# Computing K and Q of a half together in two PSUM banks, with the stationary tokens loaded once per column tile

## The chip, the cores and the metric

The kernel runs on one core of a Trainium2 chip. The metric is device time in microseconds (us), and a comparison uses fast runs only. (A run is called slow when it is over 1.5% above the fastest of the same kernel.) The record names three chips for the experiments and does not name that of the first pair. The same kernel differed between these three chips by up to 1.5% (means of the kernel before: 1052.4, 1063.3 and 1068.6 us), so every experiment is compared with runs of the kernel before that were made in the same rounds on the same chip. In the profiles PE is TensorE (matmuls), PEld its weight loads, DVE is VectorE, ACT ScalarE and POOL GpSimd; PSUM (`ps` in the traces) is the memory that the kernel's matmuls write to.

## The reference, cut to what matters

```python
# part A: recurrent attention over 64 segments, 32 heads of 128, model width 512
for s in range(64):
    h = concat([mem, x[32*s : 32*s+32]])            # 8 memory rows + 32 rows of x
    q, k, v = h @ Wq, h @ Wk, h @ Wv                # each 512 -> 32 x 128
    p = softmax(mask(q @ k.T * scale))
    o = (p @ v) @ Wo                                # 4096 -> 512
    mem = o[:8]                                     # the next segment needs these
    outs.append(o[8:])
# part B: independent local attention with a memory branch (num / den);
# out = g * A + (1 - g) * B
```

Segment s+1 needs the memory rows of segment s. The kernel therefore has one long serial loop, and it fills the gaps of part A with pieces of part B.

## The kernel before: the parts that matter

The kernel records operations per engine. Each one waits, before its first instruction, for what it reads, and for the last readers of what it overwrites. It allocates PSUM as eight banks of 512 columns (lines 247 to 250), which are tracked as resources.

```python
class Banks:
    def take(self, long=False):            # first fit in a list, oldest returned first (cut)
        ...
    def give(self, *bks):                  # back in the list when the *reading* op is recorded
        for b in bks: self.free.append(b)

# Prog._mk_deps, for a written resource:
#     deps += [r.w] and all of r.readers   (a bank: whoever last copied it out)
```

`give` is called when the program is recorded, not when the reader has run. A bank in the list can therefore still be waiting for its reader on the chip, and the op that takes it inherits that wait.

```python
A_ORDER = """
    Q1 K0 Q0 K1 V0 TK0 TQ0 S0 bP bP TQ1 TK1 bS V1 M0 S1 N0 Fc M1 PV0 E0a N1 E0b Fc PV1 E1b E1a
    W0 W1 WT bS bT Ff Ff Ff bS bP bS""".split()

def proj(bk, lhs, w_sb, b, split, reads, name):      # one pass: 16 matmuls of 512 columns
    def f(pe):
        for c in range(C):                           # 4 chunks of the width 512
            for j in range(4):                       # 4 column tiles of 32
                w = w_sb[:, c, 2048 * b:2048 * (b + 1)]
                ins = pe.matmul(pb[bk][SEG*j:SEG*(j+1), :], lhs(c), cols(w, j) if split else ...,
                                start=(c == 0), stop=(c == C - 1))
    P.op("pe", f, reads=reads, writes=[rbank[bk]], name=name)

def nat_pass(m, b, eng):                             # units K0 K1 Q0 Q1 V0 V1
    bk = B.take()
    proj(bk, lhs, w_sb, b, m != "V", ...)
    evac(eng, nat[:, b, :], pb[bk], [bk], ...)       # copy to SBUF on ACT or DVE
    B.give(bk)
```

Unit `bT` at the end of a segment runs `BAttn.chain`: matmuls of the memory branch (`bN`) into a bank `nb`, then a run of DVE operations that ends with the product `amem` read from `nb`, or, at the end of each job, a transpose copied to `oTs`.

```python
def chain(self, job, G, ob):
    nb = v.BK.take()
    P.op("pe", fn, ..., writes=[v.rbank[nb]], name="bN" + nm)
    # DVE: reciprocal, gate, adot (reads ob); then + 1e-6, reciprocal, gate ...
    P.op("dve", ... ad, T1 * rd ...); v.BK.give(ob)
    P.op("dve", ... am, T2 * rm ...)                 # "amem": the last reader of nb
    v.BK.give(nb)
```

The softmax here doesn't subtract the row's maximum and nothing guards it: scores larger than these inputs give would overflow.

## Time and profile before

The time before is 1060.99 us (median of 3 runs, 1060.31 to 1063.03). What matters, and where it is read:

| reading | value | view |
|---|---|---|
| TensorE (PE) busy | 923 of 1060 us | page, part 1 |
| one K or Q pass to the next | 0.86 us | PE timeline |
| PE gaps at one place modulo 256 instructions | 84 us in 75 gaps | worked out from the trace |
| half-rate TensorE clock | 82 us | clock records of the trace |

The page of the kernel before: the span, the engines' busy times, the granted TensorE clock in 40 slices, and the instruction queue (packets, MB, share).

```profile
span 1059.6 us, 65320 instructions
PE 923.4 (87%) x30149; PEld 565.4 (53%) x30149; DVE 558.8 (53%) x1198; ACT 586.0 (55%) x1211; POOL 229.2 (22%) x603
PEclk9998999999999989999899999999899999989999
q8 instruction: 236, 3.87, 1.5%
```

PE is the busy engine, and in all 64 segments of the trace its projections stand in the order of `A_ORDER` (Q K Q K V V). Every matmul has a weight load of its own: 30,149 of each.

Its timeline at the start of segment 23 (start, length, engine, line, operation, tiles, count):

```profile
432.77 0.39 PE L706 MATMUL ps<-QTj,KTj 32*128 32x256 bf16 x4
433.09 1.05 PE L862 MATMUL ps<-Wq_sb,hT 128*32 128x512 bf16 x16
433.97 1.04 PE L862 MATMUL ps<-Wk_sb,hT 128*32 128x512 bf16 x16
434.83 1.04 PE L862 MATMUL ps<-Wq_sb,hT 128*32 128x512 bf16 x16
435.69 1.04 PE L862 MATMUL ps<-Wk_sb,hT 128*32 128x512 bf16 x16
```

Read the starts, not the lengths: the ends of matmuls are modelled in this profile, and a pass of "1.05 us" is followed by the next after 0.86. A pass is four rounds of 512 columns in four column tiles at once, so a round takes 216 ns, although each pass also carries 16 weight loads. On PEld the loads of a round start one round ahead of their matmuls, while the round before runs: those of the fourth pass start at 435.48, its matmuls at 435.69.

DVE over the same microseconds:

```profile
432.52 0.31 DVE L868 STREAM_TRANSPOSE hT<-aW_sb 128x128 bf16<-128x128 bf16 x1 [2.54 <-ACT aW_sb L319]
432.76 0.22 DVE L786 RECIPROCAL rden<-ps 128x16 f32<-128x16 f32 x1
...
434.56 0.42 DVE L802 TENSOR_TENSOR amem<-ps,rden 128x256 f32<-128x256 f32 x1
434.91 0.68 DVE L321 CAST QN_sb<-ps 128x512 bf16<-128x512 f32 x1
```

The memory branch's chain is still running on DVE when the projections start. Its last reading of a PSUM bank, `amem`, ends at 434.98, which is 1.9 us after the first projection began. Nothing waits for it, because the pass that takes that bank is the fourth, 2.6 us in.

The second loss of the kernel, in PE's list of waits (engine, line, what it waited for: total us, times, longest) and in its timeline:

```profile
PE ps L899 <- issue: 65.1, 56, 2.3
```

```profile
414.40 1.85 PE L899 MATMUL ps<-Wo_sb,OT_sb 128*32 128x128 bf16 x109
417.93 0.46 PE L899 MATMUL ps<-Wo_sb,OT_sb 128*32 128x128 bf16 x19 [1.68 <-issue]
```

PE stops for 1.68 us in the middle of a run of matmuls that wait for nothing that the profile shows. I numbered all PE instructions of the trace, 60,503 with its semaphore instructions: such gaps fall at one place modulo 256 (positions 193 to 198), 84 us in all. The queue that the page calls `instruction` moved 236 packets of 16 KB, one for each 256 of these instructions, and no two of them overlap in time. So I read the gaps as instruction fetch, and call them fetch stalls. After the 58 stalls of over 0.6 us, the next packet starts 1.1 us after PE has resumed and takes 1.1 us, and PE resumes 1.4 us after a packet has landed (medians). Whether a stall follows went with how fast a block of 256 ran: all 43 blocks that ran in under 2.5 us were followed by one (3.5 us with it, in the mean), 27 of the 60 between 2.5 and 3.4 us, and none of the 103 over 3.6 us.

### The profile page before, as it was taken

To read this page: it belongs to the slowest core of one execution; us is meant where nothing else is said; L and a number is where in the kernel's file an instruction comes from. 1 tells how busy PE (TensorE), PEld (TensorE's weight loads), DVE (VectorE), ACT (ScalarE), POOL (GpSimd) and SP (SyncE) were. 2 spreads that over 40 slices of the span, in tenths; PEclk is the share of its full clock that TensorE was granted. 3 is DMA by queue.
4 is the path that set the end of the run, shared out by engine and by line. 5 is a ranking of instruction groups with operands and counts; after the bars stand their busy time and mean duration, and the time that the engine had idled before them with its cause. 6 is when DMAs were issued, how large, how long until landed. Compare 5 with 4: busy or idle time off the path is not lost.

```text
span 1059.6 us, 65320 instructions
## 1 busy us (share of the span) xinstructions
PE 923.4 (87%) x30149; PEld 565.4 (53%) x30149; DVE 558.8 (53%) x1198; ACT 586.0 (55%) x1211; POOL 229.2 (22%) x603
## 2 busy tenths in 40 slices
PE   7967999898988989889898999899898889988886
PEld 4434555555555545555555565555555555555544
DVE  4655555453554636465465646565464546446433
ACT  4442666565665655656565656665565666544444
POOL 6100222221222122222221222222222212211010
PEclk9998999999999989999899999999899999989999
DMA  8897000000101110000001101000111001000110
GB/s 287 265 323 256 12 13 16 17 17 12 25 14 41 38 34 20 24 15 20 20 20 44 39 22 34 14 25 15 24 40 35 22 19 39 10 14 4 40 33 9
DMA packets 65929, 52.23 MB, mean 49 GB/s; under 512 B 34288, under 2 KB 64120, under 8 KB 64120
## 3 DMA queue, kind: packets, MB, share of 16 engines
q1 hardware_dynamic: 65656, 48.06, 15.5%
q8 instruction: 236, 3.87, 1.5%
q14 instruction: 37, 0.30, 0.1%
HBM read 33.47 MB, written 14.57 MB: 45 GB/s over the span
## 4 chain that ended last, share of the span: by engine, by line
PE 72%; issue 9%; ACT 8%; DVE 6%; DMA 3%; SPq 1%; ACTq 0%; POOL 0%; DVEq 0%
PE ps L862 33%; PE ps L899 17%; PE ps L706 5%; ACT PT L714 4%; PE ps L753 4%; PE ps L582 2%; DVE LN_sb L321 2%; PE ps L1061 2%; PE ps L557 2%; ACT R_sb L1043 2%; PE ps L949 2%; ACT R_sb L1040 2%; DVE Pn_sb L1047 2%; DMA scr_pQd<-stgp 1%; DMA Wo_sb<-in_A_Wo_dram 1%
## 5 line engine op out<-in xcount | busy, mean ns | idle before, releaser
L899 PE MATMUL ps<-Wo_sb,OT_sb 128*32 128x128 bf16 x8192 | 151.8, 229 | 52.5 <-issue 51.3
L714 ACT ACTIVATE PT<-ps 128x1024 bf16<-128x1024 f32 x160 | 160.5, 1023 | 26.2 <-PE ps L706 21.9
L899 PEld LDWEIGHTS ps<-Wo_sb,OT_sb 128*32 128x32 bf16 x8192 | 127.4, 101 | 67.1 <-issue 59.2
L722 POOL TENSOR_SCALAR_AFFINE_SELECT PT<-PT 128x256 bf16<-128x256 bf16 (+1 forms) x224 | 98.8, 441 | 277.0 <-ACT PT L714 269.1
L862 PE MATMUL ps<-Wq_sb,hT 128*32 128x512 bf16 x2048 | 143.9, 396 | 2.8 <-DVE hT L868 1.9
L862 PE MATMUL ps<-Wk_sb,hT 128*32 128x512 bf16 x2048 | 139.0, 387 | 0.0
L319 ACT ACTIVATE KN_sb<-ps 128x512 bf16<-128x512 f32 x128 | 76.4, 597 | 108.6 <-PE ps L862 105.8
L868 DVE STREAM_TRANSPOSE hT<-aW_sb 128x128 bf16<-128x128 bf16 x64 | 19.9, 312 | 219.9 <-ACT aW_sb L319 219.9
L862 PE MATMUL ps<-Wv_sb,hT 128*32 128x512 bf16 x2048 | 134.9, 381 | 0.8 <-ACT V_sb L319 0.8
L319 ACT ACTIVATE OT_sb<-ps 128x320 bf16<-128x320 f32 x256 | 96.9, 430 | 55.4 <-PE ps L1070 54.4
L868 DVE STREAM_TRANSPOSE KT_sb<-KN_sb 128x512 bf16<-128x512 bf16 x128 | 88.4, 690 | 48.9 <-ACT KN_sb L319 48.6
L319 ACT ACTIVATE aW_sb<-ps 128x128 bf16<-128x128 f32 x64 | 17.8, 278 | 149.3 <-PE ps L899 146.1
L868 DVE STREAM_TRANSPOSE QT_sb<-QN_sb 128x512 bf16<-128x512 bf16 x128 | 83.5, 690 | 11.7 <-ACT QN_sb L319 10.6
L1129 POOL COPY OTL<-OT_sb 128x256 bf16<-128x256 bf16 x64 | 25.5, 398 | 295.5 <-ACT OT_sb L319 295.5
L862 PEld LDWEIGHTS ps<-Wk_sb,hT 128*32 128x32 bf16 x2048 | 57.3, 99 | 59.1 <-issue 5.7
L862 PEld LDWEIGHTS ps<-Wq_sb,hT 128*32 128x32 bf16 x2048 | 51.9, 99 | 63.3 <-issue 16.6
L321 DVE CAST V_sb<-ps 128x512 bf16<-128x512 f32 x64 | 44.3, 692 | 74.9 <-PE ps L862 74.9
L862 PEld LDWEIGHTS ps<-Wv_sb,hT 128*32 128x32 bf16 x2048 | 50.4, 96 | 54.4 <-ACT P_sb L1019 9.8
L321 DVE CAST QN_sb<-ps 128x512 bf16<-128x512 f32 x64 | 44.0, 687 | 41.4 <-PE ps L862 41.3
L706 PE MATMUL ps<-QTj,KTj 32*128 32x384 bf16 (+3 forms) x512 | 64.2, 309 | 0.0
L1040 ACT ACTIVATE R_sb<-ps 128x160 f32<-128x160 f32 x128 | 38.9, 304 | 36.6 <-PE ps L1036 36.3
L1047 DVE TENSOR_TENSOR Pn_sb<-P_sb,R_sb 128x160 bf16<-128x160 bf16 x128 | 42.6, 333 | 30.9 <-ACT R_sb L1043 21.9
(117 smaller groups left out, 1424.1 us busy)
## 6 DMA issues: line engine op xcount, KB each, us to landing
Wk_sb<-in_A_Wk_dram SPq DMA_DIRECT2D x4, 1024.0 KB, 7.0
Wq_sb<-in_A_Wq_dram SPq DMA_DIRECT2D x4, 1024.0 KB, 8.6
Wv_sb<-in_A_Wv_dram SPq DMA_DIRECT2D x4, 1024.0 KB, 8.4
Wo_sb<-in_A_Wo_dram SPq DMA_DIRECT2D x4, 1024.0 KB, 10.0
scr_vd<-V SPq DMA_DIRECT2D x16, 136.0 KB, 5.3
Vj<-scr_vd SPq DMA_DIRECT2D x32, 68.0 KB, 2.4
Wo_sb<-in_A_x_dram SPq DMA_DIRECT2D x4, 512.0 KB, 7.4
scr_kTd<-stgk SPq DMA_DIRECT2D x16, 128.0 KB, 6.5
```

The lines of the kernel that those rows point to most:

```text
L319: P.op("act", lambda a: a.activation(dst, src, ACT.Copy), reads=[v.rbank[k] for k in bks], writes=dres, name=name)
L321: P.op("dve", lambda d: d.tensor_copy(dst, src), reads=[v.rbank[k] for k in bks], writes=dres, name=name)
L706: ins = pe.matmul(v.pb[bks[x]][:, o:o + w], KT[e][r, 128 * kc:128 * (kc + 1)], QT[r, q0:q0 + w], start=True, stop=True, tile_position=(r.s ...
L714: P.op("act", lambda a: a.activation(pt[:, :, :], v.ps[:, bks[0]:bks[1] + 1, :], ACT.Exp, scale=v.SCALE_B), reads=[v.rbank[b] for b in bks ...
L722: P.op("gp", lambda g, mv=mv: g.affine_select(mv, mv, [[0, mv.shape[1]], [1, 128]], ALU.is_ge, 0.0, base=0, channel_multiplier=-1), reads= ...
L753: ins = pe.matmul(v.pb[ob][:, o:o + 17], pt[:, x, col:col + 128], V[:, kc, 17 * h:17 * (h + 1)], start=first, stop=True, skip_group_check= ...
L862: ins = pe.matmul(pb[bk][SEG * j:SEG * (j + 1), :], lhs(c), cols(w, j) if split else w[:, 512 * j:512 * (j + 1)], start=(c == 0), stop=(c ...
L868: P.op("dve", lambda d: d.transpose(dst, src), reads=reads, writes=writes, name=name)
L899: ins = pe.matmul(pb[bk][SEG * j:SEG * (j + 1), 0:128], lhs(h), cols(Wo_sb[:, h, :], j), start=(h == 0), stop=(h == H - 1))
L1040: P.op("act", lambda a: a.activation(R_sb[:, b, :], pb[bk][:, 224:384], ACT.Ln), reads=[rbank[bk]], writes=[Rs("R%d" % b)], name="ln%d_%d" ...
L1047: P.op("dve", lambda d: d.tensor_tensor(wide(Pn_sb, b)[:, :, 0:L], wide(P_sb, b)[:, :, 0:L], R_sb[:, b, :].rearrange("p (i q) -> p i q", q ...
L1129: P.op("gp", lambda gq: gq.tensor_copy(OTL[par][:, :, 8 * r:8 * r + 8], OT_sb[:, :, SEG:L]), reads=[Rs("OT%d_%d" % (c, hf)) for c in range ...
```

## The change

Its intent: K and Q of one half multiply the same stationary tokens. If both are computed together in two banks, each column tile loads its tokens once and two matmuls use them. That removes 32 of the 64 K/Q weight loads of a segment. The core of the diff:

```diff
+def matmul_again(nc, pe, first, out, rhs, start, stop):
+    m = first.ins
+    return pe.add_instruction(mybir.InstMatmult(
+        ..., ldweights=False, ..., ins=[pe.lower_ap(rhs), m.ins[1]], outs=[pe.lower_ap(out)], ...))
 A_ORDER = """
-    Q1 K0 Q0 K1 V0 TK0 TQ0 S0 bP bP ...
+    P0 P1 V0 TK0 TQ0 S0 bP bP ...
-A_ENG = dict(K0="act", K1="act", Q0="act", Q1="dve", ...
+A_ENG = dict(K0="act", K1="act", Q0="dve", Q1="act", ...
+    def proj_two(bks, lhs, w_two, b, reads, name):
+        def f(pe):
+            for c in range(C):
+                ...
+                first = [pe.matmul(pb[bks[0]][rows[j], :], lhs(c), w[0][j], ...) for j in range(4)]
+                for j in range(4):
+                    ins = matmul_again(v.nc, pe, first[j], pb[bks[1]][rows[j], :], w[1][j], ...)
+        P.op("pe", f, reads=reads, writes=[rbank[k] for k in bks], name=name)
+        def two_pass(b):
+            bks = [B.take(), B.take()]
+            proj_two(bks, lhs, (Wk_sb, Wq_sb), b, ...)
+            for m, nat, bk in (("K", KN_sb, bks[0]), ("Q", QN_sb, bks[1])):
+                evac(ENG["%s%d" % (m, b)], nat[:, b, :], pb[bk], [bk], ...)
+            B.give(*bks)
```

Note `writes=[rbank[k] for k in bks]`: the pair is one operation, and it waits for both banks before its first matmul.

More of the change, by code (lines that the diff above doesn't have):

```diff
@@ L225, in build @@
     v = NS()
+    v.nc = nc
     _, S, DM = A_x.shape
@@ L365 @@
     pass
+def matmul_again(nc, pe, first, out, rhs, start, stop):
+    m = first.ins
+    return pe.add_instruction(mybir.InstMatmult(
+        start_tensor_calc=start, stop_tensor_calc=stop, tile_size=m.tile_size, tile_position=m.tile_position, ldweights=False,
+        name=nc.get_next_instruction_name(), engine=m.engine, debug=m.debug, ins=[pe.lower_ap(rhs), m.ins[1]], outs=[pe.lower_ap(out)],
+        bass_skip_group_check=True))
 def plan_const(v):
@@ L823 @@
 A_ORDER = """
-    Q1 K0 Q0 K1 V0 TK0 TQ0 S0 bP bP TQ1 TK1 bS V1 M0 S1 N0 Fc M1 PV0 E0a N1 E0b Fc PV1 E1b E1a W0 W1 WT bS bT Ff Ff Ff
+    P0 P1 V0 TK0 TQ0 S0 bP bP TQ1 TK1 bS V1 M0 S1 N0 Fc M1 PV0 E0a N1 E0b Fc PV1 E1b E1a W0 W1 WT bS bT Ff Ff Ff
     bS bP bS""".split()
-A_ENG = dict(K0="act", K1="act", Q0="act", Q1="dve", V0="act", V1="dve", KL0="dve", KL1="dve", QL0="dve", QL1="dve", VL0="dve",
+A_ENG = dict(K0="act", K1="act", Q0="dve", Q1="act", V0="act", V1="dve", KL0="dve", KL1="dve", QL0="dve", QL1="dve", VL0="dve",
              VL1="dve", OL="act", W="act", E0a="act", E0b="act", E1a="act", E1b="act", last=0)
@@ L865, in proj @@
         P.op("pe", f, reads=reads, writes=[rbank[bk]], name=name)
+    def proj_two(bks, lhs, w_two, b, reads, name):
+        def f(pe):
+            ins = None
+            for c in range(C):
+                w = [[cols(w_sb[:, c, 2048 * b:2048 * (b + 1)], j) for j in range(4)] for w_sb in w_two]
+                rows = [slice(SEG * j, SEG * (j + 1)) for j in range(4)]
+                first = [pe.matmul(pb[bks[0]][rows[j], :], lhs(c), w[0][j], start=(c == 0), stop=(c == C - 1), skip_group_check=True)
+                         for j in range(4)]
+                for j in range(4):
+                    ins = matmul_again(v.nc, pe, first[j], pb[bks[1]][rows[j], :], w[1][j], c == 0, c == C - 1)
+            return ins
+        P.op("pe", f, reads=reads, writes=[rbank[k] for k in bks], name=name)
     def flip(dst, src, reads, writes, name):
@@ L989, in nat_pass @@
             B.give(bk)
+        def two_pass(b):
+            bks = [B.take(), B.take()]
+            proj_two(bks, lhs, (Wk_sb, Wq_sb), b, rx + [Rs("Wk"), Rs("Wq")], "KQ%d_%d" % (s, b))
+            for m, nat, bk in (("K", KN_sb, bks[0]), ("Q", QN_sb, bks[1])):
+                evac(ENG["%s%d" % (m, b)], nat[:, b, :], pb[bk], [bk], [Rs("%sN%d" % (m, b))], "%sev%d_%d" % (m, s, b))
+            B.give(*bks)
         def tr(m, b):
@@ L1133, in segment @@
         for b in range(2):
+            units["P%d" % b] = lambda b=b: two_pass(b)
             for m in "KQV":
```

## The prediction

> **What bounds it now.** TensorE, in program order: 923 of 1060 us busy (page, part 1), 72% of the chain of waits. Each of 64 segments starts with K and Q projections. A pass (16 matmuls of 512 columns, four column tiles in parallel) starts every 0.86 us, that is 4 x 216 ns. [...] the 16 weight loads of a pass (about 0.75 us on their own row) already hide under streaming.
>
> The other loss: 77 gaps, 84 us, mostly "issue" before Wo matmuls in the waits. They recur at one position modulo 256 in the order of PE instructions, beside 16 KB packets of the instruction queue (236). They are instruction fetch[...].
>
> **Removed.** 32 loads a segment, 2048 of 60,500 PE instructions. Streaming columns are unchanged, so four passes still take 3.46 us: gain about 0. Fetch: the loads vanish where PE is slow (27 ns an instruction) and stalls arise where it is dense. Shifting the trace's own stall-free instruction times to the new block positions gives 85-92 us of stalls against 84: 0 to +7 us, no gain.
>
> **Added.** Instruction order shows the first K/Q pair needs two free banks before its first matmul. Before, the first pass needed one bank, long free; the fourth, 2.6 us later, took the bank that ends the memory branch's DVE chain (the amem multiply). Now the first pair waits for it. From the trace, the end of that work minus the start of the segment's first projection: 0.4 to 1.95 us in some 24 segments (DVE amem; in a few the final-row add), under 0.1 us in some seven (oTs copy), nothing in the rest. Summed: 32 us of new PE idle, hardly absorbed.
>
> Smaller: both results of a pair are released together, so ACT evacuates K1, Q1, V0 back to back and the first softmax exp starts about 0.15-0.3 us later: 0 to +7 us. PE waits for the Q transpose before the first scores: about 2 us in all, gone. More PE idle puts more projections under the half-rate clock (16 such stretches now, each costs up to 1.7-3.4 us): 0 to +6 us.
>
> **Predicted:** 1061 + 32 + 3 (fetch) + 2 (ACT) + 2 (clock) - 5 (absorbed) = 1095 us, range 1075 to 1110. Faster by over 2%: 0.03; within 2%: 0.15; slower by over 2%: 0.82.
>
> **Right if:** PE row shows pairs of 32 matmuls taking 1.73 us, PE weight loads fall by 2048; the waits gain a line PE ps (new projection line) waiting for DVE amem of some 25 us in some 20 times, longest about 1.9 us; "issue" before Wo stays at 60-90 us; the granted clock mean is at or slightly under 0.962; DVE and ACT busy unchanged.
>
> **Wrong if:** a pass takes clearly less than 0.86 us a matrix (loads were not hidden: faster); matmuls without their own load stall the tile (slower still); fetch stalls fall by over 15 us; the DVE chain ends earlier relative to PE, or PE idle there is regained from fetch stalls in the following block (then within 2%).

That the loads hide, and that more PE idle brings more half-rate clock, were estimates when this was written; the runs below measure both.

## The result, and the profile after

The changed kernel takes 1117.42 us (median of 4 runs, 1115.79 to 1119.44) against 1060.65 us (4 runs). The ratio is 1.053, 95% interval 1.0486 to 1.0574: slower. (Here and below a ratio is formed from fast runs of the same rounds. It is not quite the ratio of the medians or means that are shown.) The outputs are correct.

The direction was forecast. The size was not: the measured time lies above the stated range of 1075 to 1110 us.

The page after:

```profile
span 1117.3 us, 63218 instructions
PE 940.6 (84%) x30127; PEld 525.0 (47%) x28101; DVE 559.4 (50%) x1198; ACT 570.5 (51%) x1211; POOL 228.1 (20%) x603
PEclk9987999898999899989899989999999999999989
q8 instruction: 228, 3.74, 1.4%
```

The 2048 loads are gone (30,149 to 28,101), and so are 8 of 236 instruction packets. The 22 missing matmuls are records that this trace lacks; a second trace of the same kernel has all of them. PE's busy time rose, though its work did not.

The start of segment 23 after, on PE:

```profile
447.51 0.39 PE L716 MATMUL ps<-QTj,KTj 32*128 32x256 bf16 x4
449.87 0.40 PE L884 MATMUL ps<-Wk_sb,hT 128*32 128x512 bf16 x4 [1.97 <-DVE amem L812]
450.09 0.40 PE L884 MATMUL ps<-Wq_sb,hT 128*32 128x512 bf16 x4
450.30 0.40 PE L884 MATMUL ps<-Wk_sb,hT 128*32 128x512 bf16 x4
```

And on DVE:

```profile
449.30 0.43 DVE L812 TENSOR_TENSOR amem<-ps,rden 128x256 f32<-128x256 f32 x1
451.82 0.69 DVE L322 CAST QN_sb<-ps 128x512 bf16<-128x512 f32 x1 [2.10 <-PE ps L884]
```

Two things are to be seen. A round of four matmuls still takes 0.215 us, with a load or without one, so nothing was gained from the loads. And the first round now stands behind `amem`: it starts 0.14 us after that product has ended, and PE has been idle for 2 us.

PE's waits after:

```profile
PE ps L923 <- issue: 66.1, 53, 2.0
PE ps L884 <- DVE amem L812: 28.2, 22, 2.1
...
PE ps L884 <- DVE aTg L991: 4.6, 4, 1.4
```

The second and the last line are new. The first is the fetch stall before Wo, unchanged.

A third thing was underrated in the prediction. In segment 30 the wait is the same, but the pairs that follow become slow:

```profile
563.34 0.40 PE L884 MATMUL ps<-Wk_sb,hT 128*32 128x512 bf16 x4 [1.96 <-DVE amem L812]
563.55 0.40 PE L884 MATMUL ps<-Wq_sb,hT 128*32 128x512 bf16 x4
563.77 0.40 PE L884 MATMUL ps<-Wk_sb,hT 128*32 128x512 bf16 x4
563.98 0.56 PE L884 MATMUL ps<-Wq_sb,hT 128*32 128x512 bf16 x4
564.29 0.68 PE L884 MATMUL ps<-Wk_sb,hT 128*32 128x512 bf16 x4
564.72 0.68 PE L884 MATMUL ps<-Wq_sb,hT 128*32 128x512 bf16 x4
```

Starts go from 0.21 us apart to 0.43. Two stretches of that kernel, segment 30's pairs and segment 23's (start and end, length, busy times with counts, then the granted clock, DMA share, GB/s):

```profile
563.30:566.70 3.40, 3.36 (x40) 0.96 (x24) 0.41 (x1) 0.35 (x1) 2.01 (x4) 0.62 0.18 34
449.80:453.20 3.40, 3.33 (x64) 1.07 (x36) 1.38 (x3) 0.60 (x1) 2.03 (x4) 1.00 0.16 32
```

In 3.4 us PE is equally "busy" in both, but at a granted clock of 0.62 it ran 40 matmuls instead of 64. The clock records hold only 1.0 and 0.5, and in each of the two traces all their changes lie within 2 ns of a grid of 3.413 us. Half-rate time rose from 82 to 115 us between these two traces (2 us of each lie after the last instruction).

Where the 57.8 us between the two traces went, by comparing starts of the same matmuls:

| part | before | after | difference |
|---|---|---|---|
| last matmul of a segment to the first K/Q matmul, 64 times | 15.8 us | 51.2 us | +35.4 |
| first to last K/Q matmul of a segment, 64 times | 222.3 us | 245.5 us | +23.2 |
| gaps at the fetch positions | 84.5 us | 89.6 us | +5.1 |
| setup ahead of the first segment | 89.4 us | 93.5 us | +4.1 |
| all else (the remainder) | | | -10.0 |

The setup is the same program in both kernels, and a later trace of the kernel before had 94 us there, so the 4.1 us are noise. The unslowed K/Q block is 3.26 us in both kernels (median), so the 23.2 us are nearly all half-rate clock. Part of the remainder may be the same clock that now hits other work less often; that is not shown. How much clock a single trace holds is partly luck: the kept second trace of the changed kernel has 98 us at half rate and 233.5 us of K/Q blocks, with a first line of 50.2 us that is nearly the same.

### The profile page after: what moved, and what is told of

Same layout as the page of the kernel before. It is cut to its first block, busy times and chain, and to the rows that moved or that the text cites. A ratio compares the mean times of both kernels' runs of the same rounds, so it can differ in the third digit from the quotient of the medians.

```text
span 1117.3 us, 63218 instructions
## 1 busy us (share of the span) xinstructions
PE 940.6 (84%) x30127; PEld 525.0 (47%) x28101; DVE 559.4 (50%) x1198; ACT 570.5 (51%) x1211; POOL 228.1 (20%) x603
## 4 chain that ended last, share of the span: by engine, by line
PE 66%; issue 10%; DVE 10%; ACT 10%; DMA 3%; POOL 0%; ACTq 0%; SPq 0%; POOLq 0%; DVEq 0%
PE ps L884 24%; PE ps L923 16%; PE ps L872 11%; ACT PT L724 4%; PE ps L716 3%; PE ps L763 3%; PE ps L592 2%; DVE LN_sb L322 2%; PE ps L1092 2%; ACT R_sb L1074 1%; DMA scr_pQd<-stgp 1%; ACT R_sb L1071 1%; DVE Pn_sb L1078 1%; PE ps L567 1%; DVE VL L322 1%
## 5 line engine op out<-in xcount | busy, mean ns | idle before, releaser
L884 PE MATMUL ps<-Wk_sb,hT 128*32 128x512 bf16 x2048 | 226.6, 421 | 36.4 <-DVE amem L812 28.2
L884 PE MATMUL ps<-Wq_sb,hT 128*32 128x512 bf16 x2048 | 225.0, 418 | 0.0
L923 PE MATMUL ps<-Wo_sb,OT_sb 128*32 128x128 bf16 x8192 | 149.1, 226 | 55.3 <-issue 55.0
L884 PEld LDWEIGHTS ps<-Wk_sb,hT 128*32 128x32 bf16 x2048 | 65.3, 105 | 209.0 <-issue 153.5
L923 PEld LDWEIGHTS ps<-Wo_sb,OT_sb 128*32 128x32 bf16 x8192 | 124.3, 100 | 70.3 <-issue 63.7
L892 DVE STREAM_TRANSPOSE QT_sb<-QN_sb 128x512 bf16<-128x512 bf16 x128 | 88.3, 690 | 66.9 <-ACT QN_sb L320 66.9
L763 PE MATMUL ps<-Vj,PT 128*128 128x17 bf16 x1280 | 50.5, 172 | 3.9 <-issue 2.9
```

The costliest lines, as they stand in the source:

```text
L763: ins = pe.matmul(v.pb[ob][:, o:o + 17], pt[:, x, col:col + 128], V[:, kc, 17 * h:17 * (h + 1)], start=first, stop=True, skip_group_check= ...
L884: first = [pe.matmul(pb[bks[0]][rows[j], :], lhs(c), w[0][j], start=(c == 0), stop=(c == C - 1), skip_group_check=True) for j in range(4)]
L892: P.op("dve", lambda d: d.transpose(dst, src), reads=reads, writes=writes, name=name)
L923: ins = pe.matmul(pb[bk][SEG * j:SEG * (j + 1), 0:128], lhs(h), cols(Wo_sb[:, h, :], j), start=(h == 0), stop=(h == H - 1))
```

## The experiments

Theory W: the loss is PE idle in the wait for the second bank, plus the half-rate clock that this idle brings; shared loads neither gain nor cost. Rival L: fewer loads are themselves the loss, because a tile stalls without its own load, or because they bring the half-rate clock.

In the tables "half rate" is the mean over the fast timed runs of twice (1 - granted clock) times the span. The fetch stalls are those of one profiled run, found by their place modulo 256; a recount of such gaps moves them by up to 3 us.

### First set, one chip; the kernel before took 1052.4 us (mean of 7), half rate 69 us

`own_loads`: pairs, order and banks as changed, every matmul with its own load.

```diff
-                    ins = matmul_again(v.nc, pe, first[j], pb[bks[1]][rows[j], :], w[1][j], c == 0, c == C - 1)
+                    ins = pe.matmul(pb[bks[1]][rows[j], :], lhs(c), w[1][j], start=(c == 0), stop=(c == C - 1), ...)
```

> Pairs and banks as in the changed kernel, but every matmul loads its own tokens again. Theory W (the early bank wait on DVE, plus the half-rate clock that follows PE idle, is the loss; the loads do not matter): 1112 us (1105 to 1120), projections still 1.73 us a pair at full clock, wait before the first pair about 35 us in all, half-rate clock 100 to 120 us, the fetch stalls back near 84 us. Rival L (fewer loads is itself the loss: a tile stalls without a load of its own[...]): near 1065 to 1075 us and half-rate clock near 82 us.

`wait_only`: the kernel before, with one thing added. The first pass of a segment also waits for the readers of the bank that would be next in the list.

```diff
+            also = []
+            if (m, b) == ("Q", 1):
+                kept = list(B.free)
+                also = list(rbank[B.take()].readers)
+                B.free[:] = kept
-            proj(bk, lhs, w_sb, b, m != "V", rx + [Rs(wr)], "%s%d_%d" % (m, s, b))
+            proj(bk, lhs, w_sb, b, m != "V", rx + [Rs(wr)], "%s%d_%d" % (m, s, b), also)
```

> The kernel before, four single passes with their own loads, but the first pass of a segment also waits for the readers of the second bank that the pair would take. W: 1111 us (1103 to 1120), wait before the first pass 31 to 36 us, half-rate clock 100 to 120 us. L: 1061 us, as before, or at most the bare 32 us of the wait with half-rate clock unchanged near 82 us (1093).

`soonest`: the changed kernel with all loads shared, but a pair takes the two banks whose readers will be done first.

```diff
+        def soonest():
+            def late(k):       # 3: read by amem, the final-row add or this segment's K/Q copy;
+                ...            # 2: by the latest part-B exp; 1: by an earlier one; 0: by others
+            bk = min((late(k), n, k) for n, k in enumerate(B.free) if k > 1)[2]
+            B.free.remove(bk)
+            return bk
-            bks = [B.take(), B.take()]
+            bks = [soonest(), soonest()]
```

> The changed kernel, all loads shared, but each pair takes the two banks that come free soonest instead of the first in the list. From the times of before, the wait falls from 32 to about 7.5 us, longest 0.5 us. W: 1079 us (1068 to 1088), half-rate clock 80 to 98 us. L: 1100 to 1117 us.

`one_pair`: only K0 and Q0 share loads; a single pass goes first, while the pair's banks come free.

```diff
-    P0 P1 V0 TK0 TQ0 S0 bP bP TQ1 ...
+    Q1 P0 K1 V0 TK0 TQ0 bP bP S0 TQ1 ...      (Q0 to ACT and Q1 to DVE as before; soonest banks)
```

> Order Q1, then K0 and Q0 as a pair with shared loads, then K1, with the soonest banks for the pair; two bP units moved ahead of S0 because Q0 is now ready later. Half of the loads are removed, expected wait about 2 us. W: 1066 us (1056 to 1076), half-rate clock 75 to 95 us. L: half of the loss, about 1089 us.

Measured:

| kernel | mean us | ratio to before | half rate | fetch stalls |
|---|---|---|---|---|
| own_loads | 1095.5 | 1.041 (1.033 to 1.048) | 89 us | 78 us |
| wait_only | 1096.6 | 1.042 (1.035 to 1.049) | 94 us | 80 us |
| soonest | 1066.6 | 1.013 (1.008 to 1.019) | 86 us | 79 us |
| one_pair | 1068.4 | 1.012 (1.005 to 1.018) | 66 us | 85 us |

PE's waits in `wait_only`:

```profile
PE ps L899 <- issue: 62.9, 55, 2.0
PE ps L862 <- DVE amem L802: 27.8, 20, 2.1
```

`wait_only` has no pair and no shared load, only the wait, and it loses 44 us, as much as `own_loads` loses. This chip was faster than the first, so my absolute times were 15 us too high; the losses against the kernel before were forecast as 50 us and came as 43 and 44 us. The half-rate time came below the forecast of 100 to 120 us too, and is 19 and 24 us above the kernel before. `soonest` keeps every shared load, takes most of the wait away, and is left with 14 us. The traces nearly close the account. The time from the last matmul of a segment to the first K/Q matmul is 15.8 us in the first trace of the kernel before, and 53.2 us in `wait_only`, 49.8 us in `own_loads` and 23.9 us in `soonest`. What each has more, plus 0.33 us for each us more at half rate (worked out below), is 45, 40 and 14 us, where 44, 43 and 14 us were measured. Rival L, which put `own_loads` and `wait_only` near the time before and `soonest` at 1100 us or more, is out as the main cause.

`one_pair` is not clean. Its time is in the range, but it still loses 16 us with no extra half-rate clock. In its trace the first scores start 0.60 us later and the second V pass starts 0.115 us later than before, in the median segment (Q0 is copied after K0 on one engine, my own edit); 64 times 0.115 is 7 us. The rest stays unexplained.

### Second set, another chip; the kernel before took 1068.6 us (mean of 7), half rate 84 us

The changed kernel again, its twin with own loads again, and `warm`: the changed kernel with useless matmuls in the pair's first, free bank while it waits for the second. They are meant to end before the wait does.

```diff
+BUSY = {17: 2, 18: 4, 19: 3, 21: 5, 23: 8, ...}         # groups of 4 matmuls, 23 segments, 121 groups
+            if b == 0 and s in BUSY:
+                def f(pe, bk=bks[0]):                     # 4 with loads, the rest with matmul_again
+                    ...
+                P.op("pe", f, reads=rx + [Rs("Wk")], writes=[rbank[bks[0]]], name="busy%d" % s)
```

> The changed kernel once more, to stand on the same chip as the next ones. Ratio to the kernel before 1.05, half-rate clock 100 to 120 us. Both theories.

> The pairs with their own loads, beside the changed kernel on one chip. If the loads do nothing, both differ by no more than the shift of the fetch stalls, 0 to 8 us in favour of own loads, and equal half-rate clock within 15 us. [...]

(The rival's figures: own loads at least 20 us less at half rate and 10 us or more faster. The means below differ by 12 us and 7 us.)

> The changed kernel with matmuls of no use in the first bank of the pair while it waits (23 segments, 121 groups of 4, some 26 us of the 35 us of wait); the first projection starts when it did. If PE idle in the wait is what brings the half-rate clock: half-rate falls to 75 to 95 us and the time is 8 to 18 us under the changed kernel's. If not: same time within 4 us and same half-rate clock.

> The kernel before, for its trace on the same chip: half-rate clock 70 to 90 us, fetch stalls 78 to 88 us, wait before the first projection as in its first trace.

| kernel | mean us | ratio to before | half rate | fetch stalls |
|---|---|---|---|---|
| after_again | 1117.6 | 1.044 (1.040 to 1.048) | 124 us | 85 us |
| own_loads_again | 1110.7 | 1.040 (1.035 to 1.044) | 112 us | 82 us |
| warm | 1108.4 | 1.038 (1.032 to 1.044) | 96 us | 90 us |
| before_again (one run) | 1057.2 | | 53 us | 88 us |

PE's waits in `own_loads_again`, and then in `warm`:

```profile
PE ps L923 <- issue: 65.2, 52, 2.0
PE ps L884 <- DVE amem L812: 25.8, 19, 2.0
```

```profile
PE ps L926 <- issue: 67.3, 53, 2.0
PE ps L875 <- DVE LN_sb L322: 10.6, 28, 0.7
...
PE ps L887 <- DVE amem L812: 1.0, 2, 0.7
```

In `warm` the `amem` line has shrunk to 1.0 us, because PE is busy with useless work up to the same moment. Half-rate time fell by 28 us, to just above the 75 to 95 us that W expected, although `warm` has some 600 instructions more than the changed kernel. The mean time fell by 9 us (standard error 4), within the 8 to 18 us that W expected; by the ratios it is only 7 us. The gain in time is thus barely clear of noise by itself, and the intervals of the two ratios overlap. The half-rate time of the runs, 109 to 144 us against 86 to 109 us, is the clearer sign. The traces that are kept of this set's four runs are of other executions than the ones in the table and in the views above. There `warm` has 81 us at half rate against 98 for the changed kernel, its K/Q blocks take 219.8 us against 233.5, and its useful work starts when it did (1.1 us earlier, summed over 64 segments), so what it gains there it gains by the clock. (Fetch stalls are 82 us against 87 in them, so `warm`'s larger figure in the table need not be its own.) The single run of `before_again` fell to 53 us at half rate, below the 70 to 90 that I expected: the half-rate time scatters from run to run, 66 to 96 us in the seven timed runs of the kernel before on this chip.

What does a microsecond at half rate cost? Over the 76 fast runs of all kernels for which a clock is on record, single runs left out, each taken relative to the mean of its kernel on its chip, the time rises by 0.33 us (standard error 0.03) per us at half rate. It would be 0.5 if all of that time went as in segment 30 above, where starts went from 0.21 to 0.43 us apart. This is a correlation between executions; only `warm` changes the clock on purpose. For `warm` it gives 28 x 0.33 = 9.2 us, and 9.2 us were measured.

### Third set, a third chip; the kernel before took 1063.3 us (mean of the 9 fast runs of 11), half rate 80 us

`soonest_again` and `soonest_own` are twins without the long wait: all loads shared, and all loads own.

> All loads shared, banks that come free soonest. Beside its twin with own loads on one chip. Ratio to the kernel before 1.013 as in its first run, half-rate clock 75 to 95 us.

> The same with every matmul loading its own tokens. If shared loads only move the fetch stalls, the two differ by under 7 us and by under 10 us of half-rate clock. If fewer loads themselves bring the half-rate clock, this one has at least 12 us less of it and is at least 6 us faster.

`sums_shared` leaves the projections as before and shares loads where PE's instructions are dense: in the softmax sums, where one block of ones multiplies two parts of P.

```diff
-                for left in range(2):
-                    for j in range(4):
-                        ins = pe.matmul(grp04(dst) if left else dst, onesb[:, rows], P left or P main, ...)
+                first = [pe.matmul(dst[j], onesb[:, SEG * j:SEG * (j + 1)], P main, ...) for j in range(4)]
+                for j in range(4):
+                    ins = matmul_again(v.nc, pe, first[j], grp04(dst[j]), P left, False, True)
```

> The kernel before, with loads shared where instructions are dense: the eight ones-matrix loads of each softmax sum become four. 512 fewer PE instructions. If instruction fetch is what the dense stretch waits for, 512 times 3.4 us / 256 = up to 7 us less: 1.000 to 0.994 of before, fetch stalls 3 to 8 us less. If loads are hidden everywhere: no change.

(The 3.4 us a block was my reading of the trace before; the 43 fast blocks there took 3.5 us with their stall.)

`wo_heads` changes the Wo product of the kernel before, to see how much dense instructions cost there: four heads at once, one in each column tile, 512 columns each, then the sum over the tiles by a short second product.

```diff
-                for j in range(4): ... pe.matmul(pb[bk][SEG*j:SEG*(j+1), 0:128], lhs(h), cols(Wo_sb[:, h, :], j), ...)
+                j = h % 4
+                ins = pe.matmul(pb[bk][SEG*j:SEG*(j+1), :], OT_sb[:, h, 0:SEG], Wo_sb[:, h, :], start=(h < 4), ...)
+        def w_sum(): ...      # copy the bank to SBUF, add its four row blocks by 4 matmuls, copy as before
-    ... W0 W1 WT bS bT Ff Ff Ff bS bP bS
+    ... W0 bS W1 bP bS WS WT bT Ff Ff Ff
```

> The kernel before, with the Wo product by heads: four heads at once in the four column tiles, 512 columns each, then one sum over the tiles through SBUF. 192 of 256 PE instructions of this stretch go, its streaming falls from 3.4 us (128 pairs at 27 ns) to 1.7 us, and one bank copy, one short product and about 1.4 us of PE idle are added. If the dense stretch is bound by instructions and their fetch: fetch stalls under 30 us, 920 to 990 us. If not, or if the idle brings the half-rate clock: 1030 us or more.

| kernel | mean us | ratio to before | half rate | fetch stalls |
|---|---|---|---|---|
| soonest_again | 1077.8 | 1.013 (1.008 to 1.018) | 94 us | 87 us |
| soonest_own | 1073.2 | 1.009 (1.005 to 1.013) | 88 us | 80 us |
| sums_shared (4 fast runs of 6) | 1049.5 | 0.987 (0.982 to 0.992) | 66 us | 76 us |
| wo_heads | 1051.9 | 0.989 (0.984 to 0.995) | 52 us | 32 us |

PE's waits in `soonest_again`:

```profile
PE ps L923 <- issue: 63.7, 57, 2.3
...
PE ps L884 <- ACT PT L724: 4.5, 10, 0.6
```

The wait of 28 us for `amem` has become 4.5 us for an exp on ACT. The twin with own loads is 4.5 us faster, has 6.5 us less at half rate and 7 us less of fetch stalls in its trace: inside the limits (7 us, 10 us) that I had set for "shared loads only move the fetch stalls", and far from a gain. The other pair of twins, `after_again` and `own_loads_again`, differs by 7 us in the same direction. So sharing the loads of the projections gained nothing, in neither pair. Whether the few us that it seems to cost are only the new place of the fetch blocks, these runs don't settle.

`sums_shared` removes only 512 loads, a quarter of what the change removed, and is 1.3% faster than the kernel before. That is more than I expected (0.994 to 1.000). Its busy times (page, part 1):

```profile
PE 914.2 (88%) x30149; PEld 552.3 (53%) x29637; DVE 559.3 (54%) x1198; ACT 585.6 (56%) x1211; POOL 228.2 (22%) x603
q8 instruction: 234, 3.83, 1.5%
```

The mean of the fast runs fell by 13.8 us. Half rate fell by 14 us, worth 5 us at 0.33; no trace of the kernel before was taken on that chip, but in its two traces the fetch stalls are 84 and 88 us, and here they are 76, which is 8 to 12 us less. That sum fits, but the trace is of the fastest of the six runs, and why the half-rate time fell was not tested. This version beats both kernels, by less than 2%.

`wo_heads` beats both as well, by 1.1%, but it missed the 920 to 990 us that I expected if instruction fetch bounds the stretch, and lies in the range of the other case (1030 us or more). With 5888 matmuls and as many loads fewer (24,261 of each), the fetch stalls fell to 32 us, near the 30 that I had said, and half rate to 52 us. I had misread the stretch, though: its 128 pairs take 2.1 us in the trace before (16 ns a pair), not 3.4. By heads it is 32 matmuls, 1.7 us at 216 ns a round of four, so by this estimate streaming gained only 0.4 us a segment. And the added copy and sum are paid in PE idle:

```profile
PE ps L1113 <- DVE QN_sb L321: 21.6, 63, 0.9
PE ps L864 <- DVE hT L870: 19.4, 37, 0.8
```

The account isn't closed: the lower fetch stalls and half rate would be worth some 60 us, these two waits take back about 40, and 11 us came.

## Why the prediction was wrong in size and right in mechanism

- *"Streaming columns are unchanged ... gain about 0"*: right. Rounds are 0.215 us apart with and without loads.
- *"85-92 us of stalls against 84"*: right, 89.6 us in the first trace.
- *"32 us of new PE idle"*: right in place and nearly in size, 35.4 us; the `amem` line has 28.2 us in 22 times, longest 2.1 (forecast: some 25 us, some 20 times, 1.9). `wait_only` shows that this wait alone, on another chip, costs 44 us, and `soonest` that most of the loss goes when most of the wait goes.
- *"hardly absorbed", then "- 5 (absorbed)"*: the 5 us were not seen. The gap before the projections grew by all of the wait and more.
- *"+ 2 (clock)", "0 to +6 us"*: **this is the term that failed.** Half-rate time rose by 33 us in the first trace and by 39 us in the means of the second set (84 to 124). At 0.33 us each that is 11 to 13 us. `warm` took 28 us of the half-rate time away again and 9 us (standard error 4) of the time with it, with the useful work starting when it did.
- With the terms as measured the sum is 1061 + 35 + 5 + 12 = 1113 us. The trace's remaining 4 us are the setup, which varied by as much between two traces of the kernel before. Of the 22 us by which the forecast was short, some 10 are the clock, 5 the absorption that did not come, 4 the setup, 3 the longer wait and 2 fetch; the 2 us forecast for ACT did not come.
- *"the first softmax exp starts later: 0 to +7 us"*: not seen. The time from the end of the K/Q block to the first product with V is 4.68 us after and 4.74 us before (mean of 64 segments).
- *"the granted clock mean is at or slightly under 0.962"*: 0.949 in the profiled run, 0.942 to 0.949 over the four. This reading was named in the prediction but not priced: a fall of 0.015 over 1100 us is 33 us at half rate.
- *"DVE and ACT busy unchanged"*: DVE is. ACT's busy time fell by 15 us, but not its work: the lengths of its instructions add up to 622 us before and 623 us after. Copies now follow each other directly on ACT, their spans overlap in the profile, and busy time counts the overlap once.

Why was the clock term too small? I had counted the wait as idle time and only guessed at its effect on the clock. The clock changed on the 3.413 us grid, so I looked at what each window of that grid held. Five traces have the early wait in full: the first trace of the changed kernel, `wait_only`, `own_loads`, and the kept traces of `after_again` and `own_loads_again`. Among the waits of over 1 us before the first projection, 28 had 1.8 us or more inside one window, and after 23 of these the next window was at half rate. Where no window held more than 1.2 us of the wait it was 0 of 25; in between, 10 of 28. So in these traces it went with the place of a 2 us wait on the grid whether half-rate clock followed, and the projections just after it paid: in the first trace after, the K/Q blocks took 23.2 us more.

In the first trace after, 7 of the 24 half-rate stretches in the segments begin after a window that holds more than 0.3 us of the wait, and in 5 of the 7 that wait is the only long idle. The other 17 come after fetch stalls or other waits, as all 15 do in the trace before. So in those 5 the wait opened a new stretch by itself, in a window without another long idle.

Before nearly all stretches in the segments PE is busy for 60% or less of the window by this profile, but no threshold is shown: in that trace 24 windows at or below 60% were followed by full clock, and in `own_loads` and `wo_heads` some at 63% to 68% were followed by half rate.

## What to carry to other kernels

Before you remove weight loads, ask what paces that stretch. Here, where rounds of 512 columns in four column tiles already started 216 ns apart, the loads cost nothing and their removal gained nothing (1.73 us for two passes with 32 loads, 1.73 us for a pair with 16). Where many short matmuls run together, fewer instructions can mean less waiting for instruction fetch: in `sums_shared` 512 loads fewer came with 8 to 12 us less of it. An operation that takes two buffers at once waits, in this program, for the later of both before its first instruction (in segment 23 the pair started 0.14 us after `amem`, and PE had been idle for 2 us), so look up which engine's work each buffer is waiting for at that moment. And a new TensorE wait can cost more than its length: here 35 us of waits brought some 12 us of half clock on top.
